# Linear attention and a GELU feed-forward layer: keys and values nine tokens to a partition, and the attention's product with q in four array tiles

## The chip, the cores and the metric

The kernel runs on one core of one Trainium2 chip. The core has five engines that run side by side and meet at semaphores: TensorE (PE in the profile; it multiplies matrices, and its weight loads are listed as PEld), VectorE (DVE), ScalarE (ACT), GpSimd (POOL) and SyncE (SP), which here issues the loads and the transposes that the DMA engines do. SBUF is the working memory of 128 partitions; PSUM is the memory that TensorE writes to[...]. The metric is the device time in microseconds (us). The kernel before takes 287.37 us (median of three runs, 287.36 to 287.77).

## The reference

Eight batches of eight heads, 576 tokens, head size 64. Linear attention with the feature map phi, then a feed-forward layer of 512, 2048 and 512 with a tanh GELU between. The 4,608 tokens are rows of the layer's input.

```python
def phi(x):
    return np.where(x > 0, x, np.exp(x) - 1.0) + 1.0
q_p, k_p = (phi(q), phi(k))
kv  = np.einsum('bhsd,bhse->bhde', k_p, v)
z   = np.sum(k_p, axis=2)
num = np.einsum('bhsd,bhde->bhse', q_p, kv)
den = np.einsum('bhsd,bhd->bhs', q_p, z)[..., None] + 1e-06
attn = num / den
# x: (batch, seq, heads*64) as 4608 rows of 512
h = x @ w_in                                  # 512 -> 2048
g = 0.5 * h * (1.0 + np.tanh(c * (h + 0.044715 * h**3)))
out = g @ w_out                               # 2048 -> 512
```

The kernel computes phi as min(exp(x), max(x + 1, 1)). It appends a column of ones to v, so that kv has 65 columns (E in the code) and the last column of the product with q is the denominator.

## The kernel before

The program is one loop over nine iterations `j` of the feed-forward layer. Iterations 0 to 7 take 512 tokens (four chunks of 128) of a batch each, and iteration 8 takes the rest, 64 tokens of each batch. An iteration has 32 slots: in 0 to 15 four matmuls of 128x512 each make one block of h, and ACT applies GELU; in 16 to 31 four matmuls each add to one of four output tiles o. (Iterations 0 and 1 have another order.) Everything else is put between slots: `at(j, slot, fn)` runs `fn` after that slot, so that the attention of batch `b` is worked out under the feed-forward layer of earlier batches.

The load buffers and the layouts. Batches 0 and 1 have k and v "paired": all 576 tokens of two heads lie over 128 partitions, nine tokens to a partition. From batch 2 the first 512 tokens of k and v lie four to a partition, and the last 64 tokens of two batches are loaded by themselves (`kr`, `vr`).

```python
J = S // HP          # 9 tokens to a partition; HP = 64, S = 576, NP = 4 pairs of heads
PAIRED = (0, 1)

def ld_tile(name, b):
    shape = [P, NP, J * D] if b in PAIRED and name != "q" else [P, H, C * D]
    ld[name, b] = pld.tile(shape, FP32, name=name + "_x", tag="ld")

def load_batch(b):
    load_main("q", q, b)
    load_main("k", k, b)
    if b % 2 == 0:
        load_rest("kr", k, b // 2)
        load_rest("vr", v, b // 2)
    load_main("v", v, b)
```

The product of k and v, in both layouts. In the paired one, contraction over 64 partitions and an output of 64 partitions use a quarter of the array, and four matmuls in a row use the four quarters. In the other one, the contraction is over 128 partitions and two matmuls use the two halves of columns.

```python
def kv_paired(b, ii, kv_of):                       # batches 0 and 1: 72 matmuls
    for j in range(J):
        for s in range(2):
            for a in range(2):
                r, u = slice(HP * a, HP * (a + 1)), 2 * ii + s
                nc.tensor.matmul(kv_of(a, ii)[HP * s : HP * (s + 1)],
                    lhsT=kp[r, j, u, :], rhs=vp[r, j, u, :], ...)

def kv_main(b, i, kv_ps):                          # batches 2 to 7: 40 matmuls
    for c in range(C + 1):                         # c == C is the rest of 64 tokens
        for s in range(2):
            h = 2 * i + s
            nc.tensor.matmul(kv_ps[HP * s : HP * (s + 1), i, :],
                lhsT=kp[:, c, h, :] if c < C else kr[:, 0, h, :],
                rhs=vp[:, c, h, :] if c < C else vr[:, h, :], ...)
```

The product with q (called n). Two heads at a time: kv of the two stands in the diagonal blocks of `kvbd`, whose other blocks are zero, so four matmuls of the whole array with 130 columns do one chunk. DVE then divides, and a DMA transposes x to be the input of the feed-forward layer.

```python
def nab_mm(qt_c, kvbd, ns, rows=slice(0, P)):
    for i in range(NP):
        nc.tensor.matmul(ns[i // 2][rows, 2 * E * (i % 2) : 2 * E * (i % 2 + 1)],
            lhsT=qt_c[:, i, rows], rhs=kvbd[:, i, :], ...)

def plan_attention(b, j, s_kv, s_n):               # called with j = b - 1, 2, (4, 6, 8, 10)
    ...
    def n(c):
        x = nab(qts[b][:, c], b)                   # nab_mm, reciprocal, multiply
        if c == 0:
            xts[b] = pt.tile([P, NP, MAIN], BF16, name="xt")
        nc.sync.dma_start_transpose(out=xt_chunk(b, c), in_=x)
    at(j, s_kv, kv)
    for c in range(C):
        at(j, s_n[c], n, c)
```

The maps of batch `b` are put under iteration b - 2: the linear parts after slot 13, the exps after slot 15, q first, then the minima. The 64 remaining q tokens of two batches (`plan_rest`, `qr`) make one chunk of their own, in slot 2 of iterations 3, 4, 5 and 7. The last output tile is evacuated in three pieces:

```python
def last_tile(g, t):
    for n, fs in enumerate((slice(0, 256), slice(256, 384), slice(384, d_model))):
        o_ps = bank("o_ps", [P, fs.stop - fs.start])
        o_mm(o_ps, g, t, range(MM), fs)
        evac(o_sb[:, 0, fs], o_ps, n % 2 == 0)      # true: ACT, false: DVE
        store_rest(t, o_sb, fs, (nc.scalar, nc.sync))
```

Of the kernel before, what the change touches and what calls it, by code (L numbers as in the profile page):

```python
# [15 lines left out]
def kernel(  # L16
# [19 lines left out]
    P = 128  # L36
# [14 lines left out]
    prest = ctx.enter_context(tc.tile_pool(name="prest", bufs=1))  # L51
# [5 lines left out]
    psm = ctx.enter_context(tc.tile_pool(name="psm", bufs=2))  # L57
    pg = ctx.enter_context(tc.tile_pool(name="pg", bufs=1))
    pout = ctx.enter_context(tc.tile_pool(name="pout", bufs=2))
    ps_b = ctx.enter_context(  # L60
# [8 lines left out]

    w_in_sb = const.tile([P, KM, d_ff], BF16, name="w_in_sb")  # L70
# [12 lines left out]
    PAIRED = (0, 1)  # L83

    def ld_tile(name, b):
        shape = [P, NP, J * D] if b in PAIRED and name != "q" else [P, H, C * D]
        ld[name, b] = pld.tile(shape, FP32, name=name + "_x", tag="ld")
# [10 lines left out]
    def load_main(name, src, b):  # L98
        ld_tile(name, b)
        nc.sync.dma_start(  # L100
            out=ld[name, b],
            in_=src[b, :, 0:MAIN, :].rearrange("h (p c) d -> p h (c d)", c=C),
        )

    def load_rest(name, src, m):
        t = (pqr if name == "qr" else prest).tile([P, H, D], FP32, name=name)
        ld[name, m] = t
        for s in range(2):
            r = t[REST * s : REST * (s + 1)]
            rows = src[2 * m + s, :, MAIN:S, :]  # L110
            if name == "qr" and m == 0:
                for a in range(2):
                    nc.sync.dma_start(
                        out=r[:, NP * a : NP * (a + 1), :],
                        in_=rows.rearrange("(u a) p d -> p a u d", a=2)[:, a],
                    )
            else:
                nc.sync.dma_start(out=r, in_=rows.rearrange("h p d -> p h d"))

    def load_batch(b):  # L120
        load_main("q", q, b)
        load_main("k", k, b)
        if b % 2 == 0:
            load_rest("kr", k, b // 2)
            load_rest("vr", v, b // 2)
        load_main("v", v, b)
# [53 lines left out]
    load_main("q", q, 3)  # L180
    load_main("k", k, 3)
# [3 lines left out]
    ident = const.tile([P, P], BF16, name="ident")  # L185
# [3 lines left out]
    vps = [const.tile([P, J * NP, E], BF16, name=f"vp{i}") for i in range(2)]  # L189
    vrs = [const.tile([P, H, E], BF16, name=f"vr{s}") for s in range(2)]  # L190
    kvbds = [const.tile([P, NP, 2 * E], BF16, name=f"kvbd{i}") for i in range(4)]
    for i in range(2):
        nc.gpsimd.memset(vps[i][:, :, D:E], 1.0)
        nc.gpsimd.memset(kvbds[i], 0.0)
    for s in range(2):
        nc.gpsimd.memset(kvbds[2 + s], 0.0)
        nc.gpsimd.memset(vrs[s], 0.0)
        nc.gpsimd.memset(vrs[s][REST * s : REST * (s + 1), :, D:E], 1.0)
# [3 lines left out]

    def vp_main(b):
        return vps[b % 2][:, 0 : C * H].rearrange("p (c h) e -> p c h e", h=H)
# [5 lines left out]
    def by_chunk(t, hs):  # L210
        return t[:, :, hs, :].rearrange("p c h d -> p h c d")
# [5 lines left out]
    def exp_of(name, b, hs=None):  # L217
        x = ld[name, b]
        hs = hs or slice(0, x.shape[1])
        if (name, b) not in exps:  # L220
            exps[name, b] = pe.tile([P, x.shape[2] // D, x.shape[1], D], BF16, name=name + "_e")
        nc.scalar.activation(  # L222
            by_chunk(exps[name, b], hs),
            x[:, hs].rearrange("p h (c d) -> p h c d", d=D),
            AF.Exp,
        )

    def linear_of(name, b, hs=None):
        x = ld[name, b]
        hs = hs or slice(0, x.shape[1])  # L230
        if (name, b) not in phi:
            phi_tiles(name, b)
        nc.vector.tensor_scalar(  # L233
            by_chunk(phi[name, b], hs),
            x[:, hs].rearrange("p h (c d) -> p h c d", d=D),
            1.0,
            1.0,
            op0=ALU.add,
            op1=ALU.max,
        )  # L240
# [14 lines left out]

    def cast_v(b, fn):
        fn(  # L257
            out=vp_main(b)[:, :, :, 0:D].rearrange("p c h d -> p h c d"),
            in_=ld["v", b].rearrange("p h (c d) -> p h c d", d=D),
        )  # L260

    def cast_vr(m):
        for s in range(2):
            r = slice(REST * s, REST * (s + 1))
            nc.vector.tensor_copy(out=vrs[s][r, :, 0:D], in_=ld["vr", m][r])
# [16 lines left out]
    def kv_main(b, i, kv_ps):  # L282
        kp, vp = phi["k", b], vp_main(b)
        kr, vr = phi["kr", b // 2], vrs[b % 2]
        for c in range(C + 1):
            for s in range(2):
                h = 2 * i + s
                nc.tensor.matmul(  # L288
                    kv_ps[HP * s : HP * (s + 1), i, :],
                    lhsT=kp[:, c, h, :] if c < C else kr[:, 0, h, :],  # L290
                    rhs=vp[:, c, h, :] if c < C else vr[:, h, :],
                    start=(c == 0),
                    stop=(c == C),
                    skip_group_check=True,
                )

    def kv_evac(b, blocks, src, fn):
        for s in range(2):
            r = slice(HP * s, HP * (s + 1))
            fn(out=kvbds[b % 4][r, blocks, E * s : E * (s + 1)], in_=src[r])  # L300

    def nab_mm(qt_c, kvbd, ns, rows=slice(0, P)):
        for i in range(NP):
            nc.tensor.matmul(  # L304
                ns[i // 2][rows, 2 * E * (i % 2) : 2 * E * (i % 2 + 1)],
                lhsT=qt_c[:, i, rows],
# [4 lines left out]
    def x_view(x, paired):  # L311
        return x.rearrange("p (u a d) -> p a u d" if paired else "p (a u d) -> p a u d", a=2, d=D)

    def nab_evac(n_ps, paired):
        n_v = n_ps[:, :, 0 : 4 * E].rearrange("p a (u e) -> p a u e", e=E)
        r = psm.tile([P, 2, NP], FP32, name="r")
        nc.vector.reciprocal(r, n_v[:, :, :, D])  # L317
        x = px.tile([P, d_model], BF16, name="x")
        nc.vector.tensor_tensor(  # L319
            x_view(x, paired),  # L320
            n_v[:, :, :, 0:D],
            r[:, :, :, None].to_broadcast([P, 2, NP, D]),
            op=ALU.mult,
        )
        return x

    def nab(qt_c, b):
        n_ps = pair_of_banks("n_ps")
        nab_mm(qt_c, kvbds[b % 4], [n_ps[:, a] for a in range(2)])
        return nab_evac(n_ps, b in PAIRED)  # L330

    def nab_in_banks(qt_c, b):
        ns = [bank("n_ps", [P, 4 * E]) for _ in range(2)]
        nab_mm(qt_c, kvbds[b % 4], ns)
        x = px.tile([P, d_model], BF16, name="x")
        for a in range(2):
            n_v = ns[a].rearrange("p (u e) -> p u e", e=E)
            r = psm.tile([P, NP], FP32, name="r1")
            nc.vector.reciprocal(r, n_v[:, :, D])
            nc.vector.tensor_tensor(  # L340
                x_view(x, b in PAIRED)[:, a],
                n_v[:, :, 0:D],
                r[:, :, None].to_broadcast([P, NP, D]),
                op=ALU.mult,
            )
        return x
# [59 lines left out]
    def first_batch():  # L406
# [50 lines left out]
        x = {0: px.tile([P, d_model], BF16, name="x")}  # L457
# [116 lines left out]
    def plan_prepare(b, s_linear, s_exp):  # L574
        rest = b % 2 == 0

        def linear(n):
            linear_of(n, b)
            if rest and n == "k":
                linear_of("kr", b // 2)  # L580

        def casts():
            cast_v(b, nc.vector.tensor_copy)
            if rest:
                cast_vr(b // 2)

        def exps_all():
            for n in "qk":
                exp_of(n, b)
            if rest:  # L590
                exp_of("kr", b // 2)

        def least_q():
            least_of("q", b)
            qts[b] = pt.tile([P, C, NP, P], BF16, name="qt")
            for c in range(C):
                nc.sync.dma_start_transpose(
                    out=qts[b][:, c],
                    in_=phi["q", b][:, c].rearrange("p h d -> p (h d)"),
                )  # L600

        def least_k():
            least_of("k", b)
            if rest:
                least_of("kr", b // 2)

        j, s = s_linear
        at(j, s, linear, "q")
        at(j, s + 1, linear, "k")
# [3 lines left out]
        at(j, s + 2, least_q)  # L613
        at(j, s + 4, least_k)

    def plan_attention(b, j, s_kv, s_n):
        def kv():
            if j == 1:
                kv_ps = pair_of_banks("kv_ps")[:, 0, 0 : NP * E].rearrange("p (i e) -> p i e", e=E)
            else:  # L620
                kv_ps = bank("kv_ps", [P, NP, E])
            for i in range(NP):
                kv_main(b, i, kv_ps)
            kv_evac(b, slice(0, NP), kv_ps, nc.vector.tensor_copy)

        def n(c):
# [181 lines left out]
```

## Time and profile before

| part | value |
|---|---|
| device time, median of 3 | 287.37 us |
| span of the profiled execution | 285.8 us |
| h matmuls 128x512 (w_in, two groups) | 478 and 63, 379 ns each by the profile |
| o matmuls 128x512 (w_out) | 547, 379 ns each |
| n matmuls 128x130 (four a chunk) | 124 of 128*128, 32 of 128*64 |
| kv matmuls 128*64 128x65 | 192 and 48 |
| kv matmuls 64*64 64x65 (batches 0 and 1) | 144 |
| DMA queue of the loads and transposes | 44.58 MB |
| rate of the DMA from 12 to 24 us, and from 24 to 42 us | 402 and 404 GB/s |

How to read it. A group's row has the line, the engine, the operation, output and inputs with their shapes, the count and the time. `128*64` in front of a matmul's shape says how much of the array it uses: rows by columns. A matmul's time in the profile runs from its start to its end, and the next one starts before that end, so what a matmul costs the engine is the distance from its start to the start of the next one. In a timeline, one line is a run of like instructions, with start, time and count; a bracket at the end is idle time and what ended it. A few per cent of the matmul records may be missing.

### The profile page before, as it was taken

To read this page: it belongs to the slowest core of one execution; us is meant where nothing else is said; L and a number is where in the kernel's file an instruction comes from. 1 tells how busy PE (TensorE), PEld (TensorE's weight loads), DVE (VectorE), ACT (ScalarE), POOL (GpSimd) and SP (SyncE) were. 2 spreads that over 40 slices of the span, in tenths; PEclk is the share of its full clock that TensorE was granted. 3 is DMA by queue.
4 is the path that set the end of the run, shared out by engine and by line. 5 is a ranking of instruction groups with operands and counts; after the bars stand their busy time and mean duration, and the time that the engine had idled before them with its cause. 6 is when DMAs were issued, how large, how long until landed. Compare 5 with 4: busy or idle time off the path is not lost.

```text
span 285.8 us, 4582 instructions
## 1 busy us (share of the span) xinstructions
PE 277.8 (97%) x1852; PEld 137.9 (48%) x1882; DVE 108.4 (38%) x180; ACT 164.1 (57%) x228; POOL 20.7 (7%) x28
## 2 busy tenths in 40 slices
PE   8999999999999999999999999999999999999994
PEld 3574455445454445544554455444544444444443
DVE  3850387444954373543256624541412010000010
ACT  4677976785966925693468636763571375036400
POOL 6147350000000000000000000000000000000000
PEclk9999999999999999999999999999999999999999
DMA  7999999977979947935996589444132200110023
GB/s 245 401 406 396 411 400 264 340 266 208 143 222 328 251 138 228 342 76 151 259 304 151 130 222 348 78 119 138 37 39 81 81 23 0 73 76 0 0 73 76
DMA packets 72084, 53.78 MB, mean 188 GB/s; under 512 B 42112, under 2 KB 64000, under 8 KB 72064
## 3 DMA queue, kind: packets, MB, share of 16 engines
q1 hardware_dynamic: 69280, 44.58, 54.2%
q10 hardware_dynamic: 2784, 8.91, 8.5%
q8 instruction: 15, 0.25, 0.3%
q14 instruction: 5, 0.04, 0.0%
HBM read 36.70 MB, written 9.44 MB: 161 GB/s over the span
## 4 chain that ended last, share of the span: by engine, by line
PE 84%; DMA 9%; SPq 2%; issue 2%; DVE 2%; POOL 1%; ACTq 0%; ACT 0%; DVEq 0%
PE o_ps L703 40%; PE h_ps L379 39%; DMA w_st<-in_moe_w_in_dram 5%; DMA k_x<-in_k_dram 4%; PE n_ps L304 3%; PE kv_ps L288 1%; SPq L134 1%; DVE k_p L246 1%; SPq L91 1%; POOL w_in_sb L146 1%; DVE vp L251 1%; ACTq L669 0%; PE t_ps L371 0%; SPq L96 0%; PE kv_ps L273 0%
## 5 line engine op out<-in xcount | busy, mean ns | idle before, releaser
L703 PE MATMUL o_ps<-w_out_sb,g 128*128 128x512 bf16 (+2 forms) x595 | 126.3, 368 | 0.7
L379 PE MATMUL h_ps<-xt,w_in_sb 128*128 128x512 bf16 (+1 forms) x550 | 116.9, 359 | 0.8 <-issue 0.2
L389 ACT ACTIVATE g<-h_ps 128x512 bf16<-128x512 f32 x144 | 84.5, 599 | 45.0 <-PE h_ps L379 41.0
L703 PEld LDWEIGHTS <-g 128*128 128x128 bf16 x608 | 57.9, 98 | 64.9
L379 PEld LDWEIGHTS <-w_in_sb 128*128 128x128 bf16 x628 | 57.1, 98 | 59.1 <-issue 0.6
L664 ACT COPY o_sb<-o_ps 128x512 f32<-128x512 f32 (+2 forms) x20 | 11.1, 561 | 61.6 <-PE o_ps L703 52.2
L664 DVE COPY o_sb<-o_ps 128x512 f32<-128x512 f32 (+1 forms) x18 | 12.0, 667 | 70.7 <-PE o_ps L703 69.7
L317 DVE RECIPROCAL r<-n_ps 128x8 f32<-128x8 f32 x33 | 6.8, 207 | 48.1 <-PE n_ps L304 48.1
L319 DVE TENSOR_TENSOR x<-n_ps,r 128x512 bf16<-128x512 f32 x33 | 22.8, 692 | 1.1
L222 ACT ACTIVATE q_e<-q_x 128x2048 bf16<-128x2048 f32 (+1 forms) x9 | 15.5, 1721 | 2.8 <-DMA q_x<-in_q_dram 2.7
L222 ACT ACTIVATE k_e<-k_x 128x2048 bf16<-128x2048 f32 (+2 forms) x9 | 15.8, 1757 | 0.8 <-DMA k_x<-in_k_dram 0.8
L246 DVE TENSOR_TENSOR q_p<-q_p,q_e 128x2048 bf16<-128x2048 bf16 (+1 forms) x9 | 9.9, 1105 | 15.0 <-ACT q_e L222 14.9
L233 DVE TENSOR_SCALAR q_p<-q_x 128x2048 bf16<-128x2048 f32 (+1 forms) x9 | 9.9, 1101 | 13.1 <-DMA q_x<-in_q_dram 13.1
L379 PE MATMUL h_ps<-xt_rest,w_in_sb 128*128 128x512 bf16 x63 | 13.9, 379 | 0.1
L233 DVE TENSOR_SCALAR k_p<-k_x 128x2048 bf16<-128x2048 f32 (+2 forms) x9 | 10.2, 1133 | 6.0 <-DMA k_x<-in_k_dram 6.0
L304 PEld LDWEIGHTS <-qt 128*128 128x128 bf16 x124 | 9.5, 98 | 6.1
L304 PE MATMUL n_ps<-kvbd,qt 128*128 128x130 bf16 x124 | 12.1, 221 | 0.0
L411 PE MATMUL w_ps<-warm 128*128 128x512 bf16 x35 | 10.4, 448 | 1.2 <-DVE warm L187 1.2
L246 DVE TENSOR_TENSOR k_p<-k_p,k_e 128x2048 bf16<-128x2048 bf16 (+2 forms) x9 | 11.0, 1227 | 0.9 <-ACT k_e L222 0.8
L222 ACT ACT_TABLE_LOAD x8 | 10.3, 1283 | 0.1
L402 ACT ACT_TABLE_LOAD x8 | 10.3, 1283 | 0.1
L257 DVE CAST vp<-v_x 128x2048 bf16<-128x2048 f32 x6 | 7.4, 1226 | 5.6 <-DMA v_x<-in_v_dram 5.6
(56 smaller groups left out, 99.8 us busy)
## 6 DMA issues: line engine op xcount, KB each, us to landing
out_dram<-o_sb ACTq DMA_DIRECT2D x16, 512.0 KB, 3.3
q_x<-in_q_dram SPq DMA_DIRECT2D x6, 1024.0 KB, 7.2
k_x<-in_k_dram SPq DMA_DIRECT2D x6, 1024.0 KB, 11.1
v_x<-in_v_dram SPq DMA_DIRECT2D x6, 1024.0 KB, 6.6
w_st<-in_moe_w_in_dram SPq DMA_DIRECT2D x3, 1024.0 KB, 13.5
w_st<-in_moe_w_out_dram SPq DMA_DIRECT2D x3, 1024.0 KB, 12.4
q_x<-in_q_dram SPq DMA_DIRECT2D x4, 512.0 KB, 8.3
k_x<-in_k_dram SPq DMA_DIRECT2D x2, 576.0 KB, 5.6
```

Of the source, the lines that this page charges most:

```text
L222: nc.scalar.activation(by_chunk(exps[name, b], hs), x[:, hs].rearrange("p h (c d) -> p h c d", d=D), AF.Exp,)
L233: nc.vector.tensor_scalar(by_chunk(phi[name, b], hs), x[:, hs].rearrange("p h (c d) -> p h c d", d=D), 1.0, 1.0, op0=ALU.add, op1=ALU.max,)
L246: nc.vector.tensor_tensor(p, p, e, op=ALU.min)
L257: fn(out=vp_main(b)[:, :, :, 0:D].rearrange("p c h d -> p h c d"), in_=ld["v", b].rearrange("p h (c d) -> p h c d", d=D),)
L304: nc.tensor.matmul(ns[i // 2][rows, 2 * E * (i % 2) : 2 * E * (i % 2 + 1)], lhsT=qt_c[:, i, rows], rhs=kvbd[:, i, :], skip_group_check=True,)
L319: nc.vector.tensor_tensor(x_view(x, paired), n_v[:, :, :, 0:D], r[:, :, :, None].to_broadcast([P, 2, NP, D]), op=ALU.mult,)
L379: nc.tensor.matmul(h_ps[:, ts], lhsT=w_in_sb[:, c, P * m : P * (m + 1)], rhs=xt[:, c, ts], start=(c == 0), stop=(c == KM - 1), skip_group_ ...
L389: nc.scalar.activation(g[:, m, :], h_ps, AF.Gelu_apprx_tanh)
L402: nc.scalar.preload_act_table_set("gelu_apprx_tanh_and_others")
L411: nc.tensor.matmul(w_ps, lhsT=warm[:, 0:P], rhs=warm)
L664: (nc.scalar.copy if on_scalar else nc.vector.tensor_copy)(dst, src)
L703: nc.tensor.matmul(o_ps, lhsT=g[:, m, P * t : P * (t + 1)], rhs=w_out_sb[:, m, fs], start=(m == 0), stop=(m == MM - 1),)
```

## The change

All batches have k and v paired now, nine tokens to a partition: one load of 2,304-byte runs in place of a main and two rest loads, no `kr` and `vr` any more, and every kv is the 72-matmul kind. From batch 4 on, n isn't done with the zero-padded `kvbd` any more but in four tiles of the array, head by head: contraction over 64, output 64 tokens. Two chunks are done in one slot, the rest with the first two (slot 5), and the kv of the next batch with the second two (slot 22), so that such tiled matmuls stand together. As a kv is wanted sooner, k is mapped before q from batch 5. The loads of later batches and the rest loads of q move to other slots. The tiles are ordered and `ident` is padded so that load buffers begin at multiples of 512 bytes in a partition. In the last tile, the third piece is evacuated by DVE instead of ACT.

```diff
+    ident = const.tile([P, P + 64], BF16, name="ident")[:, 0:P]
...
     def ld_tile(name, b):
-        shape = [P, NP, J * D] if b in PAIRED and name != "q" else [P, H, C * D]
+        shape = [P, H, C * D] if name == "q" else [P, NP, J * D]
...
     def load_batch(b):
-        load_main("q", q, b)
-        load_main("k", k, b)
-        if b % 2 == 0:
-            load_rest("kr", k, b // 2)
-            load_rest("vr", v, b // 2)
-        load_main("v", v, b)
+        load_q(b)
+        load_all_pairs("k", k, b)
+        load_all_pairs("v", v, b)
...
+    def n_quads(qt_c, bs, ns):
+        for i in range(NP):
+            for t in range(2):
+                for s in range(2):
+                    c = slice(HP * t, HP * (t + 1))
+                    nc.tensor.matmul(
+                        ns[s][c, E * i : E * (i + 1)],
+                        lhsT=qt_c[HP * s : HP * (s + 1), i, c],
+                        rhs=kv_of_head(bs[t], s, i),
+                        skip_group_check=True,
+                    )
...
+    def plan_attention(b, m_rest):
+        j = b - 1
+        def pair_of_chunks(c):
+            in_banks = nab_quads_in_banks(qts[b][:, c + 1], (b, b))
+            in_pair = nab_quads(qts[b][:, c], (b, b))
+            return (c + 1, in_banks), (c, in_pair)
+        def early():
+            chunks = pair_of_chunks(0)
+            if m_rest is not None:
+                m = m_rest
+                rest = nab_quads_in_banks(rest_qt[m], (2 * m, 2 * m + 1))
+            transposed_x(b, 1, chunks[0][1]())
+            if m_rest is not None:
+                x = rest()
+                nc.sync.dma_start_transpose(out=xt_rest[:, :, P * m : P * (m + 1)], in_=x)
+            transposed_x(b, 0, chunks[1][1]())
+        def late():
+            chunks = pair_of_chunks(2)
+            if b + 1 < B:
+                kv_ps = [bank("kv_ps", [P, 2, E]) for _ in range(2)]
+                for ii in range(2):
+                    kv_paired(b + 1, ii, lambda a, ii: kv_ps[a][:, ii, :])
+            for c, x_of in chunks:
+                transposed_x(b, c, x_of())
+            if b + 1 < B:
+                for a in range(2):
+                    nc.vector.tensor_copy(out=kvs[(b + 1) % 4][:, 2 * a : 2 * a + 2, :], in_=kv_ps[a])
+                least_q(b + 1)
+        at(j, 5, early)
+        at(j, 22, late)
...
-            evac(o_sb[:, 0, fs], o_ps, n % 2 == 0)
+            evac(o_sb[:, 0, fs], o_ps, n == 0)
...
+    plan_by_chunks(2, 1, 16, 18)
+    plan_by_chunks(3, 2, 2, 4)
...
+    at(3, 2, kv_in_pair, 4)
...
+    for b in range(4, B):
+        plan_attention(b, {4: 0, 5: 1, 6: 2, 7: 3}.get(b))
+    at(2, 23, load_batch, 5)
+    at(3, 6, load_batch, 6)
+    at(4, 6, load_batch, 7)
...
```

`plan_by_chunks` keeps batches 2 and 3 as before: a kv (now the 72-matmul kind) and then a chunk of n every other slot with `kvbd`.

## The prediction

> **What bounds the kernel now.** I read the busy times first, then the list of waits of TensorE, then the groups by shape, then the chain that ended last, and last the timeline around every small matmul.
>
> ```profile
> PE 277.8 (97%) x1852; PEld 137.9 (48%) x1882; DVE 108.4 (38%) x180; ACT 164.1 (57%) x228; POOL 20.7 (7%) x28
> ...
> PE 84%; DMA 9%; SPq 2%; issue 2%; DVE 2%; POOL 1%; ACTq 0%; ACT 0%; DVEq 0%
> ```
>
> TensorE (PE) is busy 97% of the span and is 84% of the chain. The 9% of DMA in the chain lie before 34 us. TensorE's own waits in the whole span come to 2.4 us, and after 64 us there is none:
>
> ```profile
> PE w_ps L411 <- DVE warm L187: 1.2, 1, 1.2
> PE kv_ps L273 <- DVE vp L251: 0.6, 1, 0.6
> PE n_ps L352 <- ACT kvbd L300: 0.2, 1, 0.2
> PE n_ps L352 <- issue: 0.2, 1, 0.2
> PE h_ps L379 <- issue: 0.2, 1, 0.2
> ```
>
> So the time from 64 us on is a sum of matmul start-to-start times, and only three things can change it: fewer or shorter matmul slots, a new wait, or the tail after the last matmul. The big matmuls (h and o, 128x512) start every 0.216 us and aren't touched. What is touched is the small ones between them. Busy time misleads there (the pipelined matmuls overlap), so I take starts from the timeline of TensorE:
>
> ```profile
> 40.44 0.78 PE L273 MATMUL kv_ps<-vp,k_p 64*64 64x65 bf16 x72 [0.60 <-DVE vp L251]
> 41.15 1.04 PE L703 MATMUL o_ps<-w_out_sb,g 128*128 128x512 bf16 x3
> ...
> 109.92 0.43 PE L304 MATMUL n_ps<-kvbd,qtr 128*64 128x130 bf16 x8
> ...
> 110.92 1.90 PE L379 MATMUL h_ps<-xt,w_in_sb 128*128 128x512 bf16 x7
> 112.66 0.40 PE L304 MATMUL n_ps<-kvbd,qt 128*128 128x130 bf16 x4
> 112.90 1.89 PE L379 MATMUL h_ps<-xt,w_in_sb 128*128 128x512 bf16 x8
> ...
> 198.93 0.32 PE L288 MATMUL kv_ps<-vp,k_p 128*64 128x65 bf16 x8
> ...
> 199.69 1.90 PE L379 MATMUL h_ps<-xt,w_in_sb 128*128 128x512 bf16 x7
> ...
> 228.35 0.43 PE L304 MATMUL n_ps<-kvbd,qtr 128*64 128x130 bf16 x8
> 228.72 2.55 PE L379 MATMUL h_ps<-xt,w_in_sb 128*128 128x512 bf16 x10
> ```
>
> From these starts: one n chunk (four full-array matmuls of 130 columns) takes 112.90 - 112.66 = 0.24 us of TensorE (0.236 in the unrounded starts). A kv of the 40-matmul kind takes 199.69 - 198.93 = 0.76. A rest block with such a kv takes 110.92 - 109.92 = 1.00, and a rest block alone 0.37. The kv of batch 1, which already lies nine tokens to a partition, does 72 matmuls in 41.15 - 40.44 = 0.71. Every block that doesn't use the whole array also starts late: the last full matmul before it starts 0.31 us ahead instead of 0.216, so 0.09 is added. (Seven h matmuls where eight are issued, after such blocks, is a missing record and no wait.)
>
> **What the Trainium skill says.** "TensorEngine Tiling (Array Packing)", Key Properties: tiles load weights and multiply in parallel, and a change of tiling mode drains TensorE. The trace agrees: four 64x64 tiles take one round of about 0.032 us, and going in costs the 0.09 above. Going out costs 0.13: the last of the 72 starts at 40.44 + 0.78 - 0.19 (the mean duration of that row) = 41.03, the next full one at 41.15. Then (0.71 - 0.13) / 18 rounds = 0.032 us a round.
> "TensorE: Matmul & The Clock Gate", Part 3, The mechanism: matmuls on different tiles start about 4 ns apart. The single starts of the batch 1 kv are 3 to 4 ns apart within a round, so this holds here.
> "DMA: Bandwidth & Descriptors", How a descriptor splits into AXI transactions: the pieces are counted from multiples of 256 bytes. The program before places the first load buffer at byte 70,400 of a partition, which is 256 over a multiple of 512; adding up the tiles of the changed version gives 54,784, a multiple of 512. Both are multiples of 256, so by that page nothing is gained. The packet records agree: until 42 us 1,024-byte packets take 46 ns, 2,048-byte ones 84, 2,304-byte ones 93, which is one straight line (8.4 ns plus 27.2 bytes per ns). And the four 2,304-byte runs of a partition lie in turn 256 over and on a multiple of 512, yet take the same 93.
>
> **The change part by part.** I cost a block of tiles as 0.09 in + 0.13 out + 0.032 for each round of four.
>
> 1. k and v of all batches nine tokens to a partition. A kv becomes 72 matmuls in 18 rounds: 0.22 + 0.58 = 0.80 us, where the 40 of 128*64 took 0.76 + 0.09 = 0.85. It gains 0.05 for each kv that stands alone. Gone are kr, vr and their DVE and ACT work (kr_e 1.8, vr 2.5, kr_p 2.6 us in all), none of it on the path.
>
> 2. n in four tiles from batch 4. A chunk is 16 matmuls of 64x64x65, so 4 rounds = 0.13 us instead of 0.236, but they need the 0.22 of a change of mode. Two chunks to a slot share that, the rest joins the first pair (12 rounds: 0.60), and the next kv joins the second (26 rounds: 1.05; without a kv 8 rounds: 0.48).
>
> Sum by iteration of the feed-forward part, in us of TensorE outside h and o:
> - 2: before 0.85 + 4 x 0.236 = 1.79; after 0.80 + 0.94 = 1.74
> - 3: before 1.09 + 0.94 = 2.03; after 0.80 (kv of 4 alone) + 0.60 + 1.05 = 2.45
> - 4 and 5: before 2.03 each; after 0.60 + 1.05 = 1.65 each
> - 6: before 1.79; after 0.60 + 0.48 = 1.08
> - 7: before 0.46 (last rest); after nothing
> Before 10.13, after 8.57: 1.56 less. The kv of batch 2 in iteration 1 gains the same 0.05. All of it is on the path, as TensorE waits for nothing there: -1.6 us.
>
> 3. The last store. Before, ScalarE (ACT) evacuates the third piece of the last tile, and sits behind its own DMA issue:
>
> ```profile
> 280.29 2.25 ACTq L669 DMA_DIRECT2D out_dram<-o_sb  x2
> 280.83 0.29 DVE L664 COPY o_sb<-o_ps 128x128 f32<-128x128 f32 x1 [2.00 <-PE o_ps L703]
> 282.58 0.27 ACT L664 COPY o_sb<-o_ps 128x128 f32<-128x128 f32 x1 [2.32 <-DMA out_dram<-o_sb]
> 282.87 0.50 ACTq L669 DMA_DIRECT2D out_dram<-o_sb  x1
> ```
>
> On VectorE (DVE) that copy can run when the last matmul ends, about 281.65, and be done at 281.95. But ACT's half of the store still queues behind the issue that ends at 282.53, so the last issue starts at about 282.55 and not 282.87: -0.3 us.
>
> 4. Alignment and longer runs of the loads. By the packet line above no gain until 42 us, where the DMA share is full; after that TensorE waits for no load. 0.
>
> Sum: 287.37 - 1.6 - 0.3 = 285.5.
>
> **The rivals.**
> - A new wait in the late slot. The kv of the next batch now needs k_p by slot 22 of the same iteration. In iteration 3 of the kernel before the first exp starts at 125.20 (ACT). With k first and 2.12 us for 2,304 elements (the batch 1 row) it ends at 127.3. The DVE minimum of 2,304 elements would take some 1.37 (1,224 ns for 2,048, scaled), so k_p is there at 128.7. The o matmuls start at 123.1; seven groups of four later it is 129.1, and kv comes after 8 rounds, at 129.5. Margin 0.8 us. Against it: the one such minimum in the trace took 2,190 ns, but with GpSimd at work beside it, which is idle after 43 us. If the margin fails by its own size in three iterations: +2.4 us, 287.9.
> - Late x. The x of chunks 2 and 3 is now made in slot 22 and needed at slot 32, 9 x 0.86 = 7.8 us after the block. DVE needs 0.2 + 0.69 + 2 x (0.18 + 0.42) = 2.1, each transpose occupies SP 1.3 us and lands 3.2 us after issue: some 6.5 us. It fits by over a us; six transposes in a row for the next q end before slot 5. If not, perhaps +1 us an iteration, 288 to 289.
> - The round is longer when the stationary side is q: its 64x64 weight loads last 106 ns each, as in the kv. If they showed, and a round took 0.06, the 80 rounds of n would add 2.2 us and eat the gain: 287.7. The equal shape of the batch 1 kv speaks against it.
> - The 512 bytes do help. If the loads before 42 us were 5% quicker, the 0.6 us wait for vp would go and the first batch would come some 0.3 earlier, 284.6. The equal 93 ns of the two alignments speaks against it.
>
> **Range and chances.** The sum is built on durations of the same shapes, good to perhaps 0.4 us. The waits can only add, the alignment can only subtract. Predicted 285.5, 8 in 10 between 284.3 and 287.1. To be faster by 2% it would have to come under 281.6, which needs a gain three times what TensorE has in these blocks to give; slower by 2% (293.1) needs waits of over a us in most iterations. Chances: faster 0.02, within 2% 0.95, slower 0.03.
>
> **What would show it right or wrong.** Right: in iterations 4 and 5 the first starts of h lie about 29.3 us apart instead of 29.67; an early block of 48 matmuls takes about 0.5 from its first start to the next h, a late one of 104 about 0.96; no PE wait in slot 22 or before h of slot 0; the last copy is DVE's. Wrong: a PE wait on k_p or on the transposed q or x; a round well over 0.032; packets under 46, 84 and 93 ns with the batch 1 kv starting clearly before 40.4, which would be the alignment.

## The result and the profile after

The changed kernel takes 286.16 us (median of six runs, 285.89 to 287.03) beside 287.65 us for the kernel before on the same chip: ratio 0.9949, 95% interval 0.9931 to 0.9968. A second series of the unaltered changed kernel gave 285.76 and 0.9942 (0.9927 to 0.9956). So the gain is 1.5 to 1.9 us, half to two thirds of a per cent.

The page of the changed kernel: busy time of the engines, the packets of one instruction queue, and the shares of the chain (the span is 285.2 us).

```profile
PE 278.3 (98%) x2298; PEld 135.7 (48%) x2298; DVE 106.8 (37%) x192; ACT 161.2 (57%) x222; POOL 19.0 (7%) x24
...
q8 instruction: 18, 0.29, 0.4%
...
PE 82%; DMA 10%; DVE 3%; SPq 2%; issue 1%; POOL 1%; DVEq 0%
```

TensorE is still the bound, with more and smaller matmuls in the same time. The chain has more DVE and DMA than before. TensorE's list of waits says where:

```profile
PE w_ps L412 <- DVE warm L181: 1.2, 1, 1.2
PE h_ps L380 <- DMA xt<-x: 0.7, 1, 0.7
PE kv_ps L248 <- DVE vp L237: 0.7, 1, 0.7
PE t_ps L422 <- DVE q_p L232: 0.5, 2, 0.3
PE n_ps L353 <- ACT kvbd L260: 0.2, 1, 0.2
```

The second row is new: the first h of iteration 2 waited 0.7 us for a transposed x. This traced execution took 287.03 us, the longest of its six, and is not the typical one. From iteration 3 on, none of these waits occurs.

The small matmuls in TensorE's timeline of the changed kernel (start, time, operation, count):

```profile
111.24 0.78 PE L248 MATMUL kv_ps<-vp,k_p 64*64 64x65 bf16 x72
111.95 2.76 PE L380 MATMUL h_ps<-xt,w_in_sb 128*128 128x512 bf16 x12
114.64 0.45 PE L282 MATMUL n_ps<-kv,qt 64*64 64x65 bf16 x32
114.92 0.33 PE L282 MATMUL n_ps<-kvbd,qtr 64*64 64x65 bf16 x16
115.18 0.61 PE L380 MATMUL h_ps<-xt,w_in_sb 128*128 128x512 bf16 x2
...
129.96 0.45 PE L282 MATMUL n_ps<-kv,qt 64*64 64x65 bf16 x32
130.25 0.84 PE L248 MATMUL kv_ps<-vp,k_p 64*64 64x65 bf16 x72
131.02 0.82 PE L725 MATMUL o_ps<-w_out_sb,g 128*128 128x512 bf16 x3
```

Read the starts, from the first of a block to the next big matmul. A kv takes 111.95 - 111.24 = 0.71, as predicted. An early block of 48 takes 115.18 - 114.64 = 0.54, near enough to 0.51. A late block of 104 takes 131.02 - 129.96 = 1.06, not 0.96.

The sum over iterations 2 to 7 is the time from the first h of iteration 2 to the first h of iteration 8, which no wait at the start touches. In single starts of the trace it is 175.95 us before (77.82 to 253.77). In the changed kernel it is 174.86 (79.17 to 254.03). So TensorE gained 1.1 us here, not the 1.56 of my sum; iterations 4 and 5 take 29.43 us each, where I had said about 29.3 for 29.67. The rest of the gain is behind the last matmul:

```profile
280.56 2.26 ACTq L691 DMA_DIRECT2D out_dram<-o_sb  x3
281.10 0.29 DVE L686 COPY o_sb<-o_ps 128x128 f32<-128x128 f32 x1 [2.00 <-PE o_ps L725]
281.94 0.29 DVE L686 COPY o_sb<-o_ps 128x128 f32<-128x128 f32 x1 [0.55 <-PE o_ps L725]
```

Three DMA issues of ACT now take 2.26 us from the first to the last, and no copy sits behind them. From the end of the last matmul to the end of the span (the tail) it is 3.35 us, where it was 4.17.

### The profile page after: what moved, and what is told of

The parts are those of the page before. It is cut to its first block, busy times and chain, and to the rows that moved or that the text cites. A ratio compares the mean times of both kernels' runs of the same rounds, so it can differ in the third digit from the quotient of the medians.

```text
span 285.2 us, 5408 instructions
## 1 busy us (share of the span) xinstructions
PE 278.3 (98%) x2298; PEld 135.7 (48%) x2298; DVE 106.8 (37%) x192; ACT 161.2 (57%) x222; POOL 19.0 (7%) x24
## 4 chain that ended last, share of the span: by engine, by line
PE 82%; DMA 10%; DVE 3%; SPq 2%; issue 1%; POOL 1%; DVEq 0%
PE h_ps L380 39%; PE o_ps L725 39%; DMA w_st<-in_moe_w_in_dram 5%; DMA k_x<-in_k_dram 4%; PE kv_ps L248 2%; PE n_ps L282 1%; SPq L129 1%; PE n_ps L264 1%; DMA xt<-x 1%; SPq L92 1%; DVE k_p L232 1%; POOL w_in_sb L141 1%; DVE vp L237 1%; DVE q_p L232 0%; DVE q_p L226 0%
## 5 line engine op out<-in xcount | busy, mean ns | idle before, releaser
L725 PE MATMUL o_ps<-w_out_sb,g 128*128 128x512 bf16 (+2 forms) x608 | 127.9, 368 | 0.0
L686 ACT COPY o_sb<-o_ps 128x512 f32<-128x512 f32 (+1 forms) x19 | 10.8, 575 | 65.0 <-PE o_ps L725 64.1
L295 DVE TENSOR_TENSOR x<-n_ps,r 128x256 bf16<-128x256 f32 (+1 forms) x49 | 26.4, 539 | 1.7
L294 DVE RECIPROCAL r<-n_ps 128x4 f32<-128x4 f32 (+1 forms) x49 | 9.2, 187 | 39.8 <-PE n_ps L282 30.1
L232 DVE TENSOR_TENSOR k_p<-k_p,k_e 128x2304 bf16<-128x2304 bf16 (+1 forms) x9 | 11.9, 1317 | 18.9 <-ACT k_e L218 18.8
L218 ACT ACTIVATE k_e<-k_x 128x2304 bf16<-128x2304 f32 (+1 forms) x9 | 17.1, 1904 | 0.9 <-DMA k_x<-in_k_dram 0.8
L226 DVE TENSOR_SCALAR k_p<-k_x 128x2304 bf16<-128x2304 f32 (+1 forms) x9 | 11.0, 1222 | 6.2 <-DMA k_x<-in_k_dram 6.2
L237 DVE CAST vp<-v_x 128x2304 bf16<-128x2304 f32 (+1 forms) x9 | 11.4, 1266 | 2.3 <-DMA v_x<-in_v_dram 2.2
L141 POOL CAST w_in_sb<-w_st 128x512 bf16<-128x512 f32 (+2 forms) x6 | 7.6, 1269 | 14.8 <-DMA w_st<-in_moe_w_in_dram 14.8
L147 POOL CAST w_out_sb<-w_st 128x2048 bf16<-128x2048 f32 (+2 forms) x5 | 7.1, 1427 | 8.7 <-DMA w_st<-in_moe_w_out_dram 8.7
```

Source lines behind the costliest of these rows:

```text
L141: fn(out=w_in_sb[:, :, 512 * i + fs.start : 512 * i + fs.stop], in_=w_st[True, i][:, :, fs],)
L218: nc.scalar.activation(o, i, AF.Exp)
L226: nc.vector.tensor_scalar(o, i, 1.0, 1.0, op0=ALU.add, op1=ALU.max)
L232: nc.vector.tensor_tensor(p, p, e, op=ALU.min)
L237: fn(out=vp_paired(b)[:, :, us, 0:D].rearrange("p j u d -> p u j d"), in_=ld["v", b][:, us].rearrange("p u (j d) -> p u j d", d=D),)
L295: nc.vector.tensor_tensor(x_v, n_v[heads + (slice(0, D),)], r[heads + (None,)].to_broadcast(shape + [D]), op=ALU.mult,)
```

## The experiments

Ratios are to the kernel before, with 95% intervals; "the changed kernel" as a base is the 285.76 us of the first run.

**The changed kernel again.** No edit.

> The changed kernel unaltered, as the base for the others of this series. Theory (the gain is TensorE time of the small matmuls, about 1.3 us, and the tail, about 0.5 to 0.8 us, less a new wait of 0.7 us at the start of iteration 2): ratio to the kernel before 0.993 to 0.997; in its trace the wait for the transposed x at the start of iteration 2 is there again. Rival (the 0.7 us wait and the first h 0.46 us later than before were an accident of the one traced execution): that wait is absent and the first h of 128x512 starts at 19.8 us instead of 20.25.

285.76 us, 0.9942 (0.9927 to 0.9956). In its trace the wait for x at the start of iteration 2 is gone from the list: from the first h of the second half of iteration 1 to the first h of iteration 2 it takes 15.66 us, where the changed kernel's first trace has 16.45 and the kernel before 15.65. The first h of 128x512 starts at 19.97 us, where the changed kernel's first trace has 20.25; over the traces of the kernel before it starts anywhere from 19.79 to 20.11. So the rival holds: that wait and the late start belong to single executions.

**The old tail on the changed kernel.**

```diff
-            evac(o_sb[:, 0, fs], o_ps, n == 0)
+            evac(o_sb[:, 0, fs], o_ps, n % 2 == 0)
```

> The third piece of the last tile goes back to ACT. Theory (ACT copies only after its own DMA issue is over, and the end of the span follows): the time from the end of the last matmul to the end of the span goes back from 3.3 to about 4.1 us, the kernel is 0.8 us slower than the changed one. My prediction's size for this part: 0.3 us. Rival (the issue of 1.38 us in the trace of before was an accident, such an issue takes 0.5): 0 to 0.1 us slower.

286.04 us, 0.9948 (0.9931 to 0.9964), which can't be told from the changed kernel; the medians are 0.28 us apart and decide nothing. The trace does: ACT's issue takes 0.52 and the tail 3.35 us, the same as with the copy on DVE. My theory fell, and so did my 0.3 us: in the changed kernel the tail doesn't depend on which engine copies the last piece.

**Load buffers 128 bytes past a multiple of 256.**

```diff
-    ident = const.tile([P, P + 64], BF16, name="ident")[:, 0:P]
+    ident = const.tile([P, P], BF16, name="ident")
```

> ident loses its padding, so that the load buffers begin 128 bytes past a multiple of 256 (and 384 past one of 512). Theory A (only multiples of 256 matter[...]): packets of 1,024, 2,048 and 2,304 bytes no longer take 46, 84 and 93 ns but some 4 to 9 ns more; the loads before 42 us end 2 to 3 us later, the wait for vp at the kv of batch 1 grows from 0.7 to 2 us or more, and the kernel is 1.5 to 3 us slower than the changed one. Theory B (alignment doesn't matter for these loads at all): the same packet times and the same time within 0.3 us.

288.72 us, 1.0039 (1.0024 to 1.0053), 3.0 us slower than the changed kernel. The packet records from 5 to 42 us have means of 50.6, 88.8 and 99.1 ns where the changed kernel has 46.0, 84.3 and 93.0. The windows of 12 to 24 and 24 to 42 us (last two columns: DMA share of 16 engines, GB/s):

```profile
12.00:24.00 12.00, 11.10 (x187) 8.18 (x188) 5.61 (x16) 8.44 (x18) 5.67 (x5) 1.00 1.07 379
24.00:42.00 18.00, 16.80 (x87) 7.76 (x87) 7.14 (x5) 13.55 (x16) 8.91 (x5) 1.00 1.06 381
```

And of TensorE's waits:

```profile
PE kv_ps L248 <- DVE vp L237: 1.3, 2, 1.0
...
PE h_ps L380 <- DMA xt<-x: 1.0, 1, 1.0
PE o_ps L725 <- POOL w_out_sb L147: 0.5, 1, 0.5
```

The rate falls from 402 and 404 GB/s to 379 and 381 while the DMA engines are just as full, and TensorE waits for v, for w_out and for a transposed x. Theory A holds, though the wait for v is 1.3 us and not the 2 or more that I had expected: the first h of the second half of iteration 1 comes 1.7 us later (50.17 for the 48.45 of the changed kernel's second trace), and 1.2 us more are lost in iteration 3, before the h of iteration 4 that waits for x (31.45 for 30.24). The padding keeps a loss away.

**Load buffers 256 bytes past a multiple of 512.**

```diff
-    ident = const.tile([P, P + 64], BF16, name="ident")[:, 0:P]
+    ident = const.tile([P, P + 192], BF16, name="ident")[:, 0:P]
```

> ident padded by 192 instead of 64, so that the load buffers begin 256 bytes past a multiple of 512, as in the kernel before. Theory A (only multiples of 256 matter): packet times of 46, 84 and 93 ns and the time of the changed kernel within 0.3 us. Rival (512 matters, as the change says): longer packets of 1,024 and 2,048 bytes and 0.5 us slower or more.

286.02 us, 0.9940 (0.9929 to 0.9952); packets of 46.0, 84.3 and 93.0 ns. It is 256 that matters here and not 512.

**The second rest load of q behind the transposes of x.**

```diff
-    at(1, 18, load_rest, 1)
+    at(1, 26, load_rest, 1)
```

> The second rest load of q is issued in slot 26 of iteration 1 instead of slot 18, behind the transposes of x. Theory (an issue of this load held SP for 2.6 us, so that the three transposes behind it went out late, and the first h of iteration 2 waited): the wait of 0.7 us at the start of iteration 2 goes, 0.6 us faster than the changed kernel. Rival (the DMA engines are full with the load of v of batch 3, and the transposes land late however SP orders them): the wait stays above 0.4 us.

285.62 us, 0.9935 (0.9923 to 0.9947). The wait isn't in the trace, and the transposes of x are issued in one row. But against 285.76 the gain is 0.14 us, not 0.6: the second trace of the changed kernel hadn't the wait either. SyncE's timeline shows the order of the issues in the changed kernel first; the line after the cut is that of the altered one.

```profile
69.43 1.24 SPq L624 DMA_TRANSPOSE xt<-x  x1
70.71 3.24 SPq L113 DMA_DIRECT2D qr<-in_q_dram  x2
74.05 3.88 SPq L624 DMA_TRANSPOSE xt<-x  x3
```

```profile
68.09 7.07 SPq L624 DMA_TRANSPOSE xt<-x  x4
```

The rest load held SyncE for 3.24 us in that execution. In the kernel before, the same load took 1.28 there, and the last x landed 0.14 us before its h. The place was tight already.

**Every small block in a slot of its own.**

```diff
-        at(j, 5, early)
-        at(j, 22, late)
+        at(j, 5, one(1, True))
+        if m_rest is not None:
+            at(j, 7, one_rest)
+        at(j, 9, one(0, False))
+        at(j, 18, one(3, True))
+        at(j, 20, one(2, False))
+        if b + 1 < B:
+            at(j, 22, one_kv)      # one chunk, the rest or a kv each, same matmuls
```

> From batch 4 on every chunk of n, the rest and the next kv stand in slots of their own (slots 5, 7, 9, 18, 20 and 22), with the same tiled matmuls. Theory (each visit to the tiles costs 0.22 us beside its rounds of 0.032): per iteration 2.55 us where the changed kernel has 1.78, in iteration 6 1.75 for 1.10, so 2.8 to 3.0 us slower than the changed kernel. Rival (the rounds cost what they cost and a change of mode nothing): within 0.3 us of it.

288.82 us, 1.0044 (1.0032 to 1.0056): 3.1 us slower than the changed kernel and slower than the kernel before. Iterations 3 to 6 take 31.16, 30.22, 30.23 and 29.42 us, together 121.02, where the changed kernel has 117.85. That is 15 more visits to the tiles for 3.18 us, 0.21 each. A block of one chunk by itself, and the h after it:

```profile
147.74 0.32 PE L282 MATMUL n_ps<-kv,qt 64*64 64x65 bf16 x16
148.00 1.25 PE L380 MATMUL h_ps<-xt,w_in_sb 128*128 128x512 bf16 x5
```

It takes 0.26 us (0.255 in unrounded starts), and 0.35 with the late start, so a chunk that goes to the tiles by itself costs more than the 0.236 of a full-array one. The change of mode is the price of tiles, and two chunks to a slot is what pays for it.

**Full-array chunks in the same slots.**

```diff
-            in_banks = nab_quads_in_banks(qts[b][:, c + 1], (b, b))
-            in_pair = nab_quads(qts[b][:, c], (b, b))
+            in_banks = full_in_banks(qts[b][:, c + 1], b)   # nab_mm with a zero-padded kvbd per batch
+            in_pair = full_in_pair(qts[b][:, c], b)
```

> The chunks of batches 4 to 7 are done by four full-array matmuls of 130 columns again, in the slots of the changed kernel; the rest and the kv stay in tiles. Theory (a full chunk costs 0.236 us and no change of mode, a tiled one 0.13 but needs one): early blocks 0.82 us instead of 0.63 (four times), late ones with a kv 1.27 instead of 1.15 (three times), the late one without a kv the same, so 1.1 us slower than the changed kernel. Rival (the tiles aren't quicker, what was gained came from slots and the tail): within 0.3 us.

287.14 us, 0.9988 (0.9977 to 0.9999). The early block of iteration 3:

```profile
114.42 0.63 PE L263 MATMUL n_ps<-kvbd,qt 128*128 128x130 bf16 x8
114.98 0.32 PE L281 MATMUL n_ps<-kvbd,qtr 64*64 64x65 bf16 x16
115.23 1.04 PE L379 MATMUL h_ps<-xt,w_in_sb 128*128 128x512 bf16 x4
```

It takes 0.81 us, where the tiles took 0.54 and a late start of 0.09. Iterations 3 to 6 take 30.54, 29.73, 29.73 and 28.92 us, together 118.92: 1.07 us more than with tiles, as expected. (The other 0.3 us of its time isn't explained; the traced execution, 0.8 us over the median, has a wait of 1.2 us for x at the start of iteration 2.) So the four tiles are worth 1.1 us. What is left of the change gives TensorE nothing: from the first h of iteration 2 to that of iteration 8 it takes 175.92 us, where the kernel before takes 175.95. The tail of this run is 3.35 us, as in the changed kernel.

**v of batch 1 cast by DVE alone, with the later rest load.**

```diff
-            cast_v_paired(b, halves[1], nc.gpsimd.tensor_copy)
+            cast_v_paired(b, halves[1], nc.vector.tensor_copy)
```

> The second rest load of q later, as in the run before, and both halves of v of batch 1 cast by DVE. Theory (the DVE cast of 1,152 elements takes 1.72 us because GpSimd casts the other half beside it; alone two take 2 x 0.76 = 1.5 and the wait of the kv of batch 1 falls from 0.7 to 0.5 us): 0.7 to 0.9 us faster than the changed kernel, ratio to the kernel before about 0.992. Rival (the slow cast has another cause): no more than the later rest load gives alone, 0.6 us.

285.50 us, 0.9941 (0.9926 to 0.9956). DVE's timeline of this run and of the changed kernel's first trace:

```profile
38.70 1.42 DVE L237 CAST vp<-v_x 128x1152 bf16<-128x1152 f32 x2
```

```profile
39.21 1.72 DVE L237 CAST vp<-v_x 128x1152 bf16<-128x1152 f32 x1
```

Two casts take 1.42 us without GpSimd beside them, one took 1.72 with it, and the wait for vp is gone from TensorE's list. The time is the lowest median of all, yet only 0.26 us under the changed kernel, not 0.7 to 0.9, and its interval lies on that of the changed kernel: the gain of the cast isn't shown in the time. Two of its thirteen executions took 287.26 and 287.70 us with the rest load out of the way, so something else makes single executions long too; what, no trace shows.

**The kernel before again, and the kernel before with the new tail alone.** No edit, and

```diff
-            evac(o_sb[:, 0, fs], o_ps, n % 2 == 0)
+            evac(o_sb[:, 0, fs], o_ps, n == 0)
```

> The kernel before, unaltered, for a second trace of its tail and of its first 50 us. Theory (the DMA issue of 1.38 us on ACT behind which the last copy sat belongs to this program): it is there again, and the span ends about 4.1 us after the last matmul. Rival (it was an accident of one execution, as the run with the old tail on the changed kernel suggests, where it took 0.52): the issue takes 0.5 and the span ends about 3.35 us after the last matmul.

> The kernel before with the third piece of the last tile on DVE, nothing else. Theory (the long issue on ACT belongs to the program, and the copy on DVE avoids it): span 3.35 us after the last matmul, 0.8 us faster than the kernel before, ratio about 0.997. My prediction's size: 0.3 us, 0.999. Rival (an accident): 0 to 0.1 us, 1.000.

The first: the same time (1.0002, 0.9993 to 1.0011), ACT's issue 1.18 us, the tail 3.98 us. The long issue belongs to the program before. The second: 287.43 us, 0.9994 (0.9986 to 1.0003). The tail is 3.57 us in its trace, but the issue still takes 1.19. With that issue in place the last one starts 0.75 us after the last matmul, instead of 1.24 and 1.04 in the two traces of the kernel before: 0.3 to 0.5 sooner, where my prediction had 0.3. In time this can't be told from nothing, nor from 0.3 us.

**The instruction fetch moved, in the kernel before.** What the traces of the kernel before share, and those of the changed one lack, is a 16,384-byte packet of an instruction queue at the moment of that issue. The kernel before has 15 such packets and the changed one 18; the page of the kernel before has them in this line:

```profile
q8 instruction: 15, 0.25, 0.3%
```

```diff
-        keep_warm(18)
+        keep_warm(6)
+        for _ in range(48):
+            nc.tensor.matmul(w_ps[:, 0:P], lhsT=warm[:, 0:P], rhs=warm[:, 0:P])
```

> The kernel before, with 12 of the 18 fillers of 512 columns at the start replaced by 48 of 128 columns: the same columns for TensorE to stream, but 72 more instructions (36 matmuls with their weight loads), so that what lies at one place in TensorE's instruction stream comes some 3 us earlier at the end. In both traces of the kernel before, and in that with the new tail alone, a packet of 16,384 bytes of an instruction queue begins at 281.1 to 281.3 us, as ACT's issue of 1.2 to 1.4 us does; in the traces of the changed kernel and its variants that packet comes at 274 to 276 us and the issue takes 0.5. Theory (the fetch of instructions is what makes that issue long): the packet moves to about 277 or 278 us, the issue takes 0.5, the span ends 3.35 us after the last matmul with the old tail, and the kernel is 0.6 to 0.8 us faster than the kernel before. Rival (the long issue comes from the stores themselves): the issue stays at 1.2 us or more, the time stays.

287.17 us, 0.9984 (0.9974 to 0.9994): 0.5 us faster than the kernel before (expected 0.6 to 0.8), with the attention and the tail untouched. Nothing was gained ahead of the tail: the first h of the second half of iteration 1 starts at 62.13 us (62.17 before), and that of iteration 2 at 78.34 (77.82 before). The packet now begins at 274.8 us (further away than I had worked out), ACT's issue takes 0.52 and the tail 3.32 us. The tails of the kernel before (its second trace) and of this one:

```profile
280.50 2.05 ACTq L669 DMA_DIRECT2D out_dram<-o_sb  x2
281.04 0.29 DVE L664 COPY o_sb<-o_ps 128x128 f32<-128x128 f32 x1 [2.00 <-PE o_ps L703]
282.58 0.27 ACT L664 COPY o_sb<-o_ps 128x128 f32<-128x128 f32 x1 [2.12 <-DMA out_dram<-o_sb]
```

```profile
280.82 1.39 ACTq L671 DMA_DIRECT2D out_dram<-o_sb  x2
281.37 0.29 DVE L666 COPY o_sb<-o_ps 128x128 f32<-128x128 f32 x1 [2.00 <-PE o_ps L705]
282.25 0.27 ACT L666 COPY o_sb<-o_ps 128x128 f32<-128x128 f32 x1 [1.46 <-PE o_ps L705]
```

Two issues take 2.05 us in the one and 1.39 in the other, and ACT's copy now waits for the last matmul instead of its own issue. Where the fetch falls decides the length of that issue: in the three traces with the long one, it ends 0.39 to 0.40 us after the packet does. By what path the fetch holds it wasn't tried. SyncE's issue of the same moment takes 0.47 us in all traces.

**kv ahead of n in the late slot.** The kv block is moved ahead of `pair_of_chunks(2)`.

> In the late slot the kv of the next batch is done before the two chunks of n, otherwise the changed kernel. In its trace the late block takes 1.15 us beyond the big matmuls instead of 1.05, and from about the 48th of its 104 matmuls on the starts of one round lie 8 ns apart instead of 3 to 4. Theory (the instructions come too slowly once the engine's queue is drained, whatever they are): the block still takes 1.13 to 1.17 us, and now the last matmuls of kv and all of n lie 8 ns apart; the same time. Rival (the kv matmuls are slow behind those of n, or kept by k_p or the banks): the block falls to about 1.05 us and the kernel gains 0.3 us, or it waits for k_p, which is ready at 129.4 us in iteration 3.

285.62 us, 0.9940 (0.9922 to 0.9959). Iterations 3, 4 and 5 take 30.16, 29.35 and 29.35 us instead of 30.24, 29.43 and 29.42, so the late block falls by 0.08 us, to 1.07. That is most of the 0.1 us above my estimate, and near the 1.05 of the rival. The starts within a round still go from 3 or 4 ns to 8 ns apart after some 48 matmuls, and now it is n that gets them. So the 8 ns belong to the place in a long block and not to kv, as the theory had it; but they aren't what cost the 0.08, as the rival had it. Why n ahead of kv costs that, stays open. 0.23 us in all isn't seen in the time.

## Why the prediction held, point by point

- *kv in 72 matmuls, 0.05 us less each:* right. A lone kv adds 0.80 to 0.82 us by the starts of the big matmuls around it, where the 40-matmul kind added 0.85 to 0.86.
- *n in four tiles, a block being 0.22 plus 0.032 a round:* right in its mechanism, shown from both sides by the split blocks (+3.1 us, expected 2.8 to 3.0) and the full-array chunks (+1.07 us in iterations 3 to 6, expected 1.1). The rival of longer rounds is out: at 0.06 us a round, one chunk by itself would take 0.37 us from its first start to the next h, and it takes 0.255.
- *-1.6 us of TensorE:* mis-sized; it was -1.1 from iteration 2 on. The term is the late block with a kv, put at 1.05 us and measured at 1.148 between big matmuls, three times; the early one came to 0.63 instead of 0.60, four times, and some 10 ns more are lost after each block (iteration 4 is 1.80 us longer than iteration 7, which has no blocks; its two blocks add 1.78). The split experiment's blocks of 16 and the lone kv come out at the estimate, so it is the long blocks that run over. I had read the starts of the batch 1 kv as 3 to 4 ns apart throughout; that holds for its first 47 or so, and from there on gaps of 7 to 9 ns come up in it too.
- *The tail, -0.3 us:* mis-sized, and its cause was misread. It was -0.8 between the first traces, and -0.6 against the second one of the kernel before. I saw that ACT's copy sat behind its own issue, and took the 1.38 us of that issue as given. The runs showed that this issue is long where an instruction fetch falls on it, and that the changed kernel, with more instructions (18 such packets where there were 15), has it elsewhere. The old tail on the changed kernel and the new tail on the kernel before make no difference in time that can be told from nothing; the moved fetch alone gains 0.5 us. That the change moved it off the issue was luck, and it is luck too that the two errors, 0.5 us too much and some 0.3 to 0.5 us too little, nearly cancel: the sum fits better than its terms.
- *Alignment, 0:* right, against the kernel before. The Trainium skill, "DMA: Bandwidth & Descriptors", How a descriptor splits into AXI transactions, counts pieces from multiples of 256 bytes; that is for reads, and the packets of these loads behave so on the side that is written (50.6 ns for 46.0 when it is 128 bytes off). What I didn't say is what the padding is for: without it the other edits would have put the buffers off 256, for 3.0 us.
- *A new wait for k_p in the late slot:* not there. In the changed kernel's iteration 3 its minimum took 1.36 us (estimate 1.37) and ended at 129.45 us, 0.8 before kv, as worked out.
- *x of chunks 2 and 3 too late:* not there from iteration 3 on. The wait I didn't list is that of iteration 2. It came in the changed kernel's first trace (0.7 us) and in the run with full-array chunks (1.2), and also with kv ahead of n (0.2) and in the kernel before with the moved fetch (0.4): it is in both kernels, in some executions.

## What to carry to other kernels

When the bounding engine never waits, measure blocks by the starts of the big instructions on either side. Busy time misled here: PE's went up, from 277.8 to 278.3 us, while TensorE gained 1.1. By starts the change of mode cost 0.22 us a visit, so small tiled matmuls must stand together to pay. Check that the buffers of a DMA-bound stage stay on multiples of 256 bytes whenever a tile ahead of them changes. And a gain of some tenths of a us at the end of a kernel may come from where an instruction fetch falls: move the stream by some instructions before crediting the edit.

## What the runs showed that was not expected

The DMA issue of the last tile's second piece on ACT took 1.18 to 1.38 us in the three traces in which a 16,384-byte instruction packet began within 0.1 us of it, and 0.51 or 0.52 in every trace in which that packet came elsewhere. It isn't so for every issue: two earlier store issues on ACT, in the runs with the later rest load and with the casts on DVE, began within 0.02 us of such a packet (at 138.12 and 137.81 us) and took 0.38 and 0.37, where 0.34 is usual. What sets the one in the tail apart stays open. In blocks of more than some 48 tiled matmuls, the starts inside a round go from 3 or 4 ns to about 8 ns apart, so that the starts of a round of four, first bunched within some 10 ns, are spread over all of its 33.
